# Attention, dense layer and expert layer on one core: first pair of heads loaded and split in parts, and a new table of order offsets for the attention

## The chip, the cores and the metric

The kernel runs on one core of a Trainium2 chip. The metric is the device time of one execution, in microseconds (us); lower is better. The core's engines run side by side, each through its own list of instructions in order: PE (TensorE, matrix products and transposes by an identity), DVE (VectorE), ACT (ScalarE), POOL (GpSimd) and SP (SyncE, which here only issues transfers, called DMAs).

## The reference

`q` has shape (2, 8, 1152, 64), and so have `k` and `v`: 2 batches of 8 heads. Two neighbouring rows of q are averaged, then plain softmax attention follows; its output is the input of a dense layer and that one's output the input of a layer with 8 experts.

```python
q_pool = q.reshape(B, H, S // factor, factor, D).mean(axis=3)
scores = scale * np.matmul(q_pool, k.transpose(0, 1, 3, 2))
scores = scores - np.max(scores, axis=-1, keepdims=True)
attn = np.exp(scores)
attn = attn / (np.sum(attn, axis=-1, keepdims=True) + 1e-09)
return np.matmul(attn, v).astype(np.float32)
...
h = x @ w_in
g = h - np.tanh(h)
return (g @ w_out).astype(np.float32)
```

## The kernel before

**Pairs and units.** The attention goes through 8 pairs of heads (c = 0 to 7). The 1152 pooled query rows of a pair make 9 units of 128 rows, numbered u = 9c + s; the unit s = 4 holds the last 64 rows of both heads.

**Preparation of a pair.** A DMA loads k of both heads (`ldk`), another q (`ldq`), another v (`ldv`). Each number of k and q is split into a high and a low half, since the products run in a format with fewer bits: for k a copy (`khi`) and a subtraction (`klo`) for each head, for q the addition of the two neighbouring rows (`qadd`), two copies (`qhi`) and a subtraction (`qlo`). All of these stand on POOL (helpers at L461, L470; L553). PE then transposes the halves into PSUM (`ktr` L534, `qtr` L570) and ACT copies them out (`kev`, `qev`, L459).

**A unit.** PE forms scores in three PSUM banks (`qk`, L664; there are two such sets of banks). DVE takes the row maximum (`max`, L670), ACT the exponential (`exp`, L678). POOL then splits the result into two 16-bit halves (`l` and `h`, L689), and one DMA transpose, issued from SP, puts both into the tile `pt` (`tr`, L694). For s = 3 and s = 7 the transposition is made on PE instead (`pT`, L706) with copies by ACT (L720) and DVE (L723).

**AV.** When a pair's transposes have landed, PE multiplies `pt` with v in six groups of 24 matmuls (`av{c}.{g}.{part}`, L736): g = 0 reads the columns of units 0, 1, 2, 4, 5, 6 of the pair, g = 1 those of units 2 to 4 and 6 to 8. There is one tile `pt`: the transposes of the next pair write over the same columns, so each waits for the AV groups that read them. After each g DVE scales the result (`xf`, L800), and POOL splits it for the next layer (`xhi`, `xlo`).

**Order.** Every operation is recorded with a due time `at`, to which the table `ORDER` adds an offset by the kind of operation. `Plan.run` then goes through all operations with assumed durations, gives each an engine, a place in the engine's list and its buffers, and writes the lists down; at run time nothing is reordered. Weights of the dense layer are loaded and split in the same lists (L851 to L880). The dense layer (L906, L963) and the experts come behind the attention.

Of the kernel before, what the change touches and what calls it, by code (L numbers as in the profile page):

```python
# [17 lines left out]
ALU = mybir.AluOpType  # L18
# [139 lines left out]
ORDER = {"av": -5.5, "c0": 12, "c1": 5, "c2": -6.5, "c3": -1.5, "cabs": -13.5, "kev": -2, "khi": -1.5, "klo": -6.5,  # L158
         "l": -4, "ldk": 0.5, "ldq": 2, "ldv": 1.5, "ldw": 3.5, "max": 0.5, "pth": 1.5, "ptl": 3, "qadd": -1.5,
         "qev": 13.5, "qhi": -2.5, "qk": -0.5, "qlo": -12, "qtr": 3, "rbe": -2, "rbt": 0.5, "rbz": 1, "rd": 8.5,  # L160
         "rec": 7.5, "rze": -4, "sv": 3, "tr": 18, "vbc": 3, "vhi": 1.5, "vlo": 11, "vsc": -2.5, "vsum": 0.5, "vtr": 6,
         "xf": -4.5, "xhi": -5, "xlo": -1.5}
# [248 lines left out]
def d1(n):  # L411
    return 0.12 + 0.00108 * n
# [6 lines left out]
def p2(n):  # L419
    return 0.2 + 0.0025 * n  # L420
# [6 lines left out]
class Kernel:  # L427
# [45 lines left out]

    def attention(self):
        nc, P = self.nc, self.P
        V = P.v
# [39 lines left out]

        def prep_k(n, need):
            raw = kraw[n // 2]

            def rw():  # L520
                return V(raw)[:, n % 2]

            sp = P.sb([KT, 2, D], F32R, f"ksp{n}")
            t = kT[n] = P.sb([S], F32R, f"kT{n}")
            P.op(self.copy_alts(lambda: V(sp)[:, :, 0, :], rw, KT * D, CFG["khi"], slow=True), r=[raw], w=[(sp, 0)],
                 at=need - CFG["kpr"], name=f"khi{n}")
            P.op(self.sub_alts(lambda: V(sp)[:, :, 1, :], rw, lambda: V(sp)[:, :, 0, :].bitcast(F32), KT * D, CFG["klo"]),
                 r=[raw, (sp, 0)], w=[(sp, 1)], at=need - CFG["kpr"] + 1, name=f"klo{n}")
            for g in range(3):
                ps = P.ps(1, F32R, f"kps{n}.{g}")  # L530

                def pe_(g=g, ps=ps):
                    for i in range(3):
                        nc.tensor.transpose(out=V(ps)[:, 0, i * 128:(i + 1) * 128],  # L534
                                            in_=V(sp)[:, 3 * g + i].rearrange("p a d -> p (a d)"), identity=ident_r)

# [5 lines left out]

        def prep_q(c, need):
# [15 lines left out]
            P.op(self.sub_alts(lambda: V(t)[:, :, 1, :], lambda: V(s), lambda: V(t)[:, :, 0, :].bitcast(F32), n, CFG["qlo"]),
                 r=[s, (t, 0)], w=[(t, 1)], at=need - CFG["qpr"] + 2, name=f"qlo{c}")  # L560
# [980 lines left out]
def sel(name, alts):  # L1541
# [9 lines left out]
           avg=2.7, av0=10.5, avs=2.0, fin=11.5, t1=21, hp=8.1, wld=8, wcv=20, wsp=17, cv0=60, cvs=25, fn0=2, hch=6, xadd='ppvppvppv', xof=6,  # L1551
# [56 lines left out]
```

## Time and profile before

| | |
|---|---|
| time, 3 runs | 654.37 us median, 652.66 to 654.85 |
| the profiled execution | 655.12 us, of it the span in the trace 653.1 us |
| PE busy over the span | 588.3 us, 90% |
| DVE, ACT, POOL busy | 373.9, 349.8 and 348.0 us |
| chain that ended last | issue 15%, one DMA behind the dense layer 5% |

The profile's span runs from the first to the last instruction of the program. Busy time of an engine leaves out issuing, branches and waits. A row of the timeline gives the start, the time to the last end of the merged instructions, the engine, the line of the code, output and input with their shapes, the count, and in brackets the idle time before it and the instruction that ended it.

### The profile page before, as it was taken

To read this page: it belongs to the slowest core of one execution; us is meant where nothing else is said; L and a number is where in the kernel's file an instruction comes from. 1 tells how busy PE (TensorE), PEld (TensorE's weight loads), DVE (VectorE), ACT (ScalarE), POOL (GpSimd) and SP (SyncE) were. 2 spreads that over 40 slices of the span, in tenths; PEclk is the share of its full clock that TensorE was granted. 3 is DMA by queue.
4 is the path that set the end of the run, shared out by engine and by line. 5 is a ranking of instruction groups with operands and counts; after the bars stand their busy time and mean duration, and the time that the engine had idled before them with its cause. 6 is when DMAs were issued, how large, how long until landed. Compare 5 with 4: busy or idle time off the path is not lost. (4 is left out here: it accounts for less than half of the span.)

```text
span 653.1 us, 10491 instructions
## 1 busy us (share of the span) xinstructions
PE 588.3 (90%) x3840; PEld 471.9 (72%) x3840; DVE 373.9 (57%) x579; ACT 349.8 (54%) x641; POOL 348.0 (53%) x303
## 2 busy tenths in 40 slices
PE   3879898979898979999999999899999959999993
PEld 2767787867786868888899999799989456338331
DVE  1687767695777686898879896854554021101100
ACT  4886877776868786856775766544441100120011
POOL 7996959696969588976446365522232100110111
PEclk9979999998999999999999999899998979999997
DMA  7799989998999695999935123344277843595000
GB/s 217 167 200 204 218 195 204 219 212 172 192 214 211 128 176 124 162 349 356 411 131 178 34 67 95 119 139 129 67 215 249 224 128 129 178 371 190 22 24 13
DMA packets 172371, 114.82 MB, mean 176 GB/s; under 512 B 135470, under 2 KB 144686, under 8 KB 172048
## 3 DMA queue, kind: packets, MB, share of 16 engines
q1 hardware_dynamic: 169152, 109.37, 64.5%
q0 software_dynamic: 1680, 3.81, 1.9%
q10 hardware_dynamic: 1472, 0.79, 0.6%
q8 instruction: 37, 0.61, 0.4%
q14 instruction: 30, 0.25, 0.1%
HBM read 66.22 MB, written 16.15 MB: 126 GB/s over the span
## 5 line engine op out<-in xcount | busy, mean ns | idle before, releaser
L470 POOL TENSOR_TENSOR b<-b,b 128x512 fp32r<-128x512 f32 (+2 forms) x88 | 149.9, 1715 | 97.8 <-ACT b L459 80.6
L689 POOL TENSOR_SCALAR b<-b 128x1152 f16<-128x1152 uint16 (+1 forms) x110 | 131.5, 1216 | 42.1 <-ACT b L678 37.8
L963 PE MATMUL psum<-b,b 128*128 128x512 f32 x432 | 118.3, 400 | 4.3 <-POOL b L470 3.7
L670 DVE CUSTOM_DVE_ANT_1 b<-psum,na 128x1152 f16<-128x1152 f32 x72 | 97.5, 1355 | 42.5 <-PE psum L664 34.8
L906 PE MATMUL psum<-b,b 128*128 128x384 f32 x576 | 116.0, 340 | 1.0 <-DVE b L723 1.0
L906 PEld LDWEIGHTS psum<-b,b 128*128 128x128 f32 x576 | 103.8, 190 | 8.3 <-DVE b L723 1.3
L678 ACT ACTIVATE b<-psum,b 128x1152 int32<-128x1152 f32 (+1 forms) x72 | 88.0, 1222 | 39.3 <-DVE b L670 36.2
L664 PE MATMUL psum<-b,b 128*128 128x384 f32 x384 | 87.5, 365 | 18.0 <-ACT b L678 17.3
L963 PEld LDWEIGHTS psum<-b,b 128*128 128x128 f32 x432 | 79.5, 189 | 17.9 <-POOL b L470 5.4
L664 PEld LDWEIGHTS psum<-b,b 128*128 128x128 f32 x384 | 67.3, 197 | 26.6 <-ACT b L678 21.5
L459 ACT ACTIVATE b<-psum 128x384 fp32r<-128x384 f32 (+3 forms) x119 | 60.2, 540 | 46.1 <-PE psum L963 14.6
L736 PE MATMUL psum<-b,b 128*64 128x288 f16 x1152 | 81.1, 293 | 3.7 <-DMA b<-b 1.4
L736 PEld LDWEIGHTS <-b 128*64 128x64 f16 x1152 | 64.9, 112 | 15.7 <-issue 10.4
L459 ACT ACTIVATE b<-b 128x512 fp32r<-128x512 f32 (+1 forms) x56 | 39.7, 720 | 48.3 <-DVE b L937 25.8
L1270 POOL DMA_INDIRECT out_dram<-b,b x8 | 7.3, 916 | 80.2 <-DVE b L1424 40.2
L1424 DVE SCALAR_TENSOR_TENSOR b<-psum,b,b 64x512 f32<-64x512 f32 x8 | 5.9, 742 | 70.1 <-ACT b L1421 70.1
L1404 ACT ACTIVATE b<-psum 128x512 f32<-128x512 f32 x8 | 4.8, 597 | 58.6 <-PE psum L1400 58.6
L878 DVE SCALAR_TENSOR_TENSOR b<-b,b 128x512 uint32<-128x512 uint32 x32 | 34.7, 1101 | 0.2
L929 DVE SCALAR_TENSOR_TENSOR b<-psum,b 128x768 f32<-128x768 f32 x24 | 22.8, 952 | 17.3 <-ACT b L924 8.2
L880 DVE SCALAR_TENSOR_TENSOR b<-b,b 128x512 uint32<-128x512 uint32 x32 | 32.4, 1026 | 0.2
L1389 PE MATMUL psum<-b,b 128*64 128x512 f32 x128 | 30.6, 602 | 2.0 <-ACT b L459 1.4
L723 DVE SCALAR_TENSOR_TENSOR b<-psum,b 128x384 f16<-128x384 f32 x48 | 25.0, 551 | 12.1 <-ACT b L720 12.1
(130 smaller groups left out, 803.2 us busy)
## 6 DMA issues: line engine op xcount, KB each, us to landing
b<-in_moe_w_dram SPq DMA_DIRECT2D x64, 512.0 KB, 6.0
b<-in_moe_w_in_dram SPq DMA_DIRECT2D x32, 256.0 KB, 4.4
b<-in_moe_w_out_dram SPq DMA_DIRECT2D x16, 512.0 KB, 7.5
xs<-b SPq DMA_DIRECT2D x6, 771.0 KB, 9.9
b<-in_k_dram SPq DMA_DIRECT2D x8, 576.0 KB, 4.2
b<-in_q_dram SPq DMA_DIRECT2D x8, 576.0 KB, 5.4
b<-in_v_dram SPq DMA_DIRECT2D x8, 576.0 KB, 4.2
xd<-b SPq DMA_DIRECT2D x2, 2304.0 KB, 18.0
```

The source lines that it names most:

```text
L459: "a": ("act", (a_ps if ps else a_sb)(n), lambda: nc.scalar.activation(out=dst(), in_=src(), func=ACTF.Copy)),
L470: "p": ("pool", p2(n), lambda: nc.gpsimd.tensor_tensor(out=dst(), in0=a(), in1=b(), op=ALU.subtract)),
L664: nc.tensor.matmul(out=V(S_)[:, j, 0:CB], lhsT=lhsT, rhs=rhs[:, j * CB:(j + 1) * CB], start=(m == 0), stop=(m == len(mm) - 1))
L670: P.op([("dve", 1.43, lambda: nc.vector.tensor_tensor_reduce(out=V(junk), in0=V(S_)[:, :, 0:CB], in1=self.na[:, 3:4].unsqueeze(2).to_broad ...
L678: P.op([("act", 1.4, lambda: nc.scalar.activation(out=V(p).rearrange("p (a e) -> p a e", a=3), in_=V(S_)[:, :, 0:CB], func=ACTF.Exp, bias= ...
L689: P.op([("pool", p1(S), lambda a=a, src=src, by=by: nc.gpsimd.tensor_scalar(out=V(hl)[:, a], in0=src(), scalar1=by, scalar2=0.0, op0=ALU.m ...
L736: nc.tensor.matmul(out=V(ps)[i * D:(i + 1) * D, 0, 0:half], lhsT=V(v16[2 * c + i])[:, j, vl, :], rhs=V(pt)[:, hl * KT + j, i * SQ + g * ha ...
L878: (0.9, lambda: nc.vector.scalar_tensor_tensor(out=V(t), in0=lo(), scalar=29, in1=V(t), op0=ALU.logical_shift_right, op1=ALU.bitwise_or)),
L880: (0.9, lambda: nc.vector.scalar_tensor_tensor(out=V(t), in0=hi(), scalar=0x80000000, in1=V(t), op0=ALU.bitwise_and, op1=ALU.bitwise_or)),
L906: nc.tensor.matmul(out=V(h)[:, a, 0:384], lhsT=w, rhs=V(xx)[:, dk, sl], start=(n == 0), stop=(n == 11))
L963: nc.tensor.matmul(out=V(ps)[:, 0, :], lhsT=V(g[gi, blk, i][gl])[:, a, sl], rhs=V(wo[2 * gi + i, a])[:, wl, :], start=(i == 0 and a == 0 a ...
L1389: nc.tensor.matmul(out=V(h)[i * SM:(i + 1) * SM, 0, :], lhsT=V(xT[e // 2])[:, e % 2, k], rhs=V(w[e, k])[:, i * FH:(i + 1) * FH], start=(k ...
```

## The change

For pair 0 alone, k is loaded by one DMA for each head and q by two (blocks 0 to 4, then 5 to 8), issued k, q, k, q. Head 0 of k and the first part of q no longer go through POOL alone: copies on ACT, addition and subtraction on DVE. Pair 0's transposed tiles are copied out of PSUM by DVE or ACT. The table `ORDER` is replaced, and five numbers of the due times (`av0`, `avs`, `fin`, `cv0`) with it, which applies to all pairs.

```diff
-ORDER = {"av": -5.5, "c0": 12, "c1": 5, ... "qadd": -1.5, ... "xlo": -1.5}
+ORDER = {"av": -4, "c0": 15.5, "c1": -5.5, ... "qadd": -3, ... "xlo": -1}
...
+    def add_alts(self, dst, a, b, n, engs="vp"):
+        nc = self.nc
+        c = {
+            "v": ("dve", d1(n), lambda: nc.vector.tensor_tensor(out=dst(), in0=a(), in1=b(), op=ALU.add)),
+            "p": ("pool", p2(n), lambda: nc.gpsimd.tensor_tensor(out=dst(), in0=a(), in1=b(), op=ALU.add)),
+        }
+        return [c[e] for e in engs]
...
+            if c == 0:
+                for i in range(2):
+                    P.op([("dma", 1.45, lambda i=i: nc.sync.dma_start(
+                        out=V(raw)[:, i].rearrange("p j d -> p (j d)"), in_=k[b, h + i].rearrange("(p j) d -> p (j d)", j=KT)))],
+                        w=[(raw, i)], at=need - CFG["kld"] + 3 * i, name=f"ldk{c}.{i}")
+                return
...
+            khi, klo, kev = ("a", "v", "va") if n == 0 else (CFG["khi"], CFG["klo"], CFG["kev"])
...
+            first = c == 0
+            for pt, (t0, t1) in enumerate(((0, NF + 1), (NF + 1, NS)) if first else ((0, NS),)):
...
+                early = first and pt == 0
+                qadd, qhi, qlo = ("v", "a", "v") if early else (CFG["qadd"], CFG["qhi"], CFG["qlo"])
...
-                P.op([("pe", len(blocks) * 0.105, pe_)], r=[t], w=[ps], at=at, name=f"qtr{c}.{gi}")
+                P.op([("pe", len(blocks) * 0.105, pe_)], r=tr, w=[ps], at=at, name=f"qtr{c}.{gi}")
...
-           avg=2.7, av0=10.5, avs=2.0, fin=11.5, t1=21, hp=8.1, wld=8, wcv=20, wsp=17, cv0=60, ...
+           avg=2.7, av0=9.5, avs=3, fin=12, t1=21, hp=8.1, wld=8, wcv=20, wsp=17, cv0=55, ...
```

The order of instructions changes on every engine from the first load to the last AV. On PE the lists of both kernels agree again from the dense layer on, but for a few neighbours.

On PE, at the start of the program, before the change: b_115 and b_117 are the halves of k of heads 0 and 1, b_143 those of q of pair 0, b_130 and b_177 the transposed k and q, b_164 and b_231 the same of pair 1.

```order
L534 MATMUL psum<-ident_r,b_115 128x128 x9
L534 MATMUL psum<-ident_r,b_117 128x128 x9
L605 MATMUL psum<-ident,b_141 2x128
L570 MATMUL psum<-ident_r,b_143 128x128 x18
L664 MATMUL psum<-b_130,b_177 128x384 x6
L627 MATMUL psum<-b_184,ones 128x4
L664 MATMUL psum<-b_130,b_177 128x384 x6
```

The same place with the change: b_115 and b_143 are the halves of k of heads 0 and 1, b_133 those of q, b_125 and b_149 the transposed k and q.

```order
L549 MATMUL psum<-ident_r,b_115 128x128 x9
L594 MATMUL psum<-ident_r,b_133 128x128 x10
L688 MATMUL psum<-b_125,b_149 128x384 x12
L549 MATMUL psum<-ident_r,b_143 128x128 x6
L688 MATMUL psum<-b_125,b_149 128x384 x6
L594 MATMUL psum<-ident_r,b_133 128x128 x8
L629 MATMUL psum<-ident,b_192 2x128
```

Head 1 of k, the second part of q and the step for v (L605, now L629) have gone from ahead of the first scores to between the units.

On POOL, from the first load to the halves of unit 0 (L689), before: the list goes through k and q of pair 0 (b_111, b_113) and of pair 1 (b_137, b_159) and then reaches unit 0.

```order
L461 TENSOR_SCALAR b_115<-b_111 128x9x64
L461 TENSOR_SCALAR b_117<-b_111 128x9x64
L470 TENSOR_TENSOR b_115<-b_111,b_115 128x9x64
L553 TENSOR_TENSOR b_122<-b_113 128x576
L470 TENSOR_TENSOR b_117<-b_111,b_117 128x9x64
L461 TENSOR_SCALAR b_143<-b_122 128x9x64 x2
L470 TENSOR_TENSOR b_143<-b_122,b_143 128x9x64
...
L461 TENSOR_SCALAR b_231<-b_198 128x9x64 x2
L470 TENSOR_TENSOR b_231<-b_198,b_231 128x9x64
L689 TENSOR_SCALAR b_261<-b_241 128x1152 x2
L689 TENSOR_SCALAR b_285<-b_264 128x1152 x2
```

With the change (L713 is L689 of before, L478 stands for L553): head 1 of k and the second part of q, then unit 0; pair 1 (b_204, b_184) follows between the units.

```order
L461 TENSOR_SCALAR b_143<-b_111 128x9x64
L470 TENSOR_TENSOR b_143<-b_111,b_143 128x9x64
L478 TENSOR_TENSOR b_128<-b_113 128x256
L461 TENSOR_SCALAR b_133<-b_128 128x4x64 x2
L470 TENSOR_TENSOR b_133<-b_128,b_133 128x4x64
L713 TENSOR_SCALAR b_202<-b_186 128x1152 x2
L713 TENSOR_SCALAR b_221<-b_200 128x1152 x2
L478 TENSOR_TENSOR b_241<-b_204 128x576
L713 TENSOR_SCALAR b_252<-b_233 128x1152 x2
L461 TENSOR_SCALAR b_280<-b_241 128x9x64 x2
L470 TENSOR_TENSOR b_280<-b_241,b_280 128x9x64
L461 TENSOR_SCALAR b_301<-b_184 128x9x64
```

Eight instructions of pair 1 that stood ahead of unit 0 now stand behind it, up to unit 6.

On SP, the transposes of pair 2 up to the one before its AV, before: b_298 is the tile `pt`, the first two rows belong to units 18 and 19, the last four to units 20, 22, 23 and 24.

```order
L694 DMA_TRANSPOSE b_298<-b_900 128x18x128
L694 DMA_TRANSPOSE b_298<-b_944 128x18x128
L851 DMA b_1151<-in_moe_w_in_dram 128x256 x2
L596 DMA b_1184<-in_v_dram 128x2x576
L694 DMA_TRANSPOSE b_298<-b_1091 128x18x128
L694 DMA_TRANSPOSE b_298<-b_1182 128x18x128
L694 DMA_TRANSPOSE b_298<-b_1243 128x18x128
L694 DMA_TRANSPOSE b_298<-b_1268 128x18x128
```

The same six transposes with the change (L718 is L694 of before, b_266 the tile `pt`).

```order
L718 DMA_TRANSPOSE b_266<-b_884 128x18x128
L718 DMA_TRANSPOSE b_266<-b_919 128x18x128
L571 DMA b_1141<-in_q_dram 128x9x128
L718 DMA_TRANSPOSE b_266<-b_1021 128x18x128
L718 DMA_TRANSPOSE b_266<-b_1130 128x18x128
L718 DMA_TRANSPOSE b_266<-b_1183 128x18x128
L718 DMA_TRANSPOSE b_266<-b_1231 128x18x128
```

Two loads of weights and one of v have left the place ahead of the last four transposes; one load of q stands there.

## Rows read from the trace of the kernel before

**Rows 1.** Waits of PE up to 290 us: total us, times, longest us.

```profile
PE psum L664 <- ACT b L678: 17.6, 21, 1.9
PE psum L736 <- DMA b<-b: 1.4, 2, 0.8
```

**Rows 2.** Busy us of each engine by stage, then PE's granted clock, DMA share, GB/s.

```profile
0.00:17.10 17.10, 6.40 (x37) 5.02 (x38) 2.72 (x12) 7.04 (x16) 13.67 (x38) 1.00 0.72 208
17.10:51.40 34.30, 27.99 (x158) 24.86 (x157) 27.78 (x43) 28.57 (x58) 33.25 (x29) 0.90 0.90 191
...
286.40:494.90 208.50, 204.22 (x1039) 182.86 (x1040) 153.25 (x197) 116.91 (x185) 97.52 (x57) 0.99 0.50 170
```

**Rows 3.** The same columns, stretches from a pair's last AV group to the next pair's first.

```profile
68.52:83.55 15.03, 11.43 (x78) 9.71 (x77) 11.35 (x23) 13.87 (x28) 13.69 (x13) 1.00 1.07 202
...
166.44:179.63 13.19, 11.01 (x77) 9.80 (x75) 9.55 (x21) 12.86 (x28) 12.56 (x13) 0.95 1.03 185
...
261.52:276.30 14.78, 13.72 (x81) 12.77 (x81) 13.31 (x20) 13.14 (x26) 14.17 (x11) 1.00 0.98 169
sum 104.54, PE 84.64 PEld 75.03 DVE 83.25 ACT 90.93 POOL 98.55; mean PE 12.09 PEld 10.72 DVE 11.89 ACT 12.99 POOL 14.08
```

**Rows 4.** The same columns, stretches from a pair's first AV group to its last.

```profile
51.44:68.52 17.08, 16.45 (x184) 13.37 (x183) 11.78 (x19) 9.63 (x19) 11.63 (x11) 1.00 0.96 215
...
sum 130.37, PE 128.32 PEld 107.97 DVE 84.63 ACT 88.01 POOL 88.16; mean PE 16.04 PEld 13.50 DVE 10.58 ACT 11.00 POOL 11.02
```

**Rows 5.** Timeline of PE from 160 to 170 us, end of pair 3's AV.

```profile
164.78 1.66 PE L736 MATMUL psum<-b,b 128*64 128x288 f16 x24
```

**Rows 6.** Timeline of SP from 164 us, transposes of pair 4.

```profile
166.60 11.25 SPq L694 DMA_TRANSPOSE b<-b  x4
```

**Rows 7.** The instructions of L694 from 166.7 to 177.8 us, their landing.

```profile
DMA to landing us min/median/max: 4.7/4.8/4.9
```

**Rows 8.** Timeline of all engines, from the first load to AV of pair 0.

```profile
1.29 0.49 SPq L513 DMA_DIRECT2D b<-in_k_dram  x1
...
5.59 1.31 POOL L461 TENSOR_SCALAR b<-b 128x576 fp32r<-128x576 f32 x2 [2.46 <-DMA b<-in_k_dram]
...
8.31 1.00 PE L534 MATMUL psum<-ident_r,b 128*128 128x128 f32 x6 [8.31 <-POOL b L470]
...
17.10 2.25 PE L664 MATMUL psum<-b,b 128*128 128x384 f32 x6
...
20.98 1.65 DVE L642 SCALAR_TENSOR_TENSOR b<-b,b,b 128x576 f16<-128x576 f32 x1
...
22.90 7.24 POOL L689 TENSOR_SCALAR b<-b 128x1152 f16<-128x1152 uint16 x6 [0.88 <-ACT b L678]
...
23.83 0.82 DVE L642 SCALAR_TENSOR_TENSOR b<-b,b,b 128x576 f16<-128x576 f32 x1
...
38.40 5.53 POOL L689 TENSOR_SCALAR b<-b 128x1152 f16<-128x1152 uint16 x4
...
54.87 1.31 PE L664 MATMUL psum<-b,b 128*128 128x384 f32 x6
```

**Rows 9.** Groups by line and form up to 290 us: busy us, mean ns, idle before.

```profile
L670 DVE CUSTOM_DVE_ANT_1 b<-psum,na 128x1152 f16<-128x1152 f32 x72 | 97.5, 1355 | 42.5 <-PE psum L664 34.8 <-ACT b L678 2.7 <-ACT b L873 2.6
L678 ACT ACTIVATE b<-psum,b 128x1152 int32<-128x1152 f32 x56 | 68.4, 1221 | 25.9 <-DVE b L670 22.9 <-POOL b L689 1.2 <-POOL b L470 1.2
L689 POOL TENSOR_SCALAR b<-b 128x1152 f16<-128x1152 uint16 x56 | 67.8, 1210 | 42.1 <-ACT b L678 37.8 <-issue 3.2 <-DMA b<-b 0.3
L470 POOL TENSOR_TENSOR b<-b,b 128x576 fp32r<-128x576 f32 x32 | 46.6, 1457 | 0.9
L461 POOL TENSOR_SCALAR b<-b 128x576 fp32r<-128x576 f32 x40 | 27.3, 693 | 5.4 <-DMA b<-in_k_dram 2.8 <-DVE b L800 1.8 <-POOL b L689 0.7
L459 ACT ACTIVATE b<-psum 128x512 fp32r<-128x512 f32 x32 | 18.7, 597 | 2.4 <-PE psum L570 2.1 <-DVE b L642 0.2
L601 ACT ACTIVATE b<-b 128x576 f16<-128x576 f32 x16 | 10.9, 684 | 0.0
```

More of the change, by code (lines that the diff above doesn't have):

```diff
@@ L155, in cost @@
     return d
[L158 to L162, printed above, removed]
+ORDER = {"av": -4, "c0": 15.5, "c1": -5.5, "c2": -9.5, "c3": 0.5, "cabs": -14.5, "exp": 3, "h": 1.5, "kev": -2,
+         "khi": 5, "klo": -9.5, "ktr": -1, "l": -2.5, "ldk": 1, "ldq": 1.5, "ldv": 1.5, "ldw": -6, "pth": 4.5,
+         "ptl": 4.5, "qadd": -3.5, "qev": 18.5, "qhi": 10, "qk": -2.5, "qlo": -8, "qtr": 11.5, "rbe": -5, "rbt": -1.5,
+         "rbz": -1, "rd": 7.5, "rec": -3, "rze": -6, "sv": 13.5, "tr": 13.5, "vbc": 3.5, "vlo": 9.5, "vsc": -5.5,
+         "vsum": -5.5, "vtr": 6, "xf": -6.5, "xhi": 13, "xlo": -1}
 def kind(name):
@@ L524, in prep_k @@
             t = kT[n] = P.sb([S], F32R, f"kT{n}")
-            P.op(self.copy_alts(lambda: V(sp)[:, :, 0, :], rw, KT * D, CFG["khi"], slow=True), r=[raw], w=[(sp, 0)],
+            khi, klo, kev = ("a", "v", "va") if n == 0 else (CFG["khi"], CFG["klo"], CFG["kev"])
+            P.op(self.copy_alts(lambda: V(sp)[:, :, 0, :], rw, KT * D, khi, slow=True), r=[(raw, n % 2)], w=[(sp, 0)],
                  at=need - CFG["kpr"], name=f"khi{n}")
-            P.op(self.sub_alts(lambda: V(sp)[:, :, 1, :], rw, lambda: V(sp)[:, :, 0, :].bitcast(F32), KT * D, CFG["klo"]),
-                 r=[raw, (sp, 0)], w=[(sp, 1)], at=need - CFG["kpr"] + 1, name=f"klo{n}")
+            P.op(self.sub_alts(lambda: V(sp)[:, :, 1, :], rw, lambda: V(sp)[:, :, 0, :].bitcast(F32), KT * D, klo),
+                 r=[(raw, n % 2), (sp, 0)], w=[(sp, 1)], at=need - CFG["kpr"] + 1, name=f"klo{n}")
             for g in range(3):
@@ L565, in prep_q @@
                 ps = P.ps(1, F32R, f"qps{c}.{gi}")
+                tr = [(t, (int(gi > 2) if first else None, j)) for j in range(3)]
                 blocks = [(g[0], s_ + g[1] * (NF + 1)) for s_ in range(NF)] if g != "z" else [(0, NF), (1, NF)]
@@ L573, in prep_q @@
                 at = need - CFG["qtr"] + gi
-                P.op([("pe", len(blocks) * 0.105, pe_)], r=[t], w=[ps], at=at, name=f"qtr{c}.{gi}")
+                P.op([("pe", len(blocks) * 0.105, pe_)], r=tr, w=[ps], at=at, name=f"qtr{c}.{gi}")
                 if g != "z":
                     P.op(self.copy_alts(lambda g=g: V(qt)[:, g[0], g[1] * NF:(g[1] + 1) * NF, :].rearrange("p a e -> p (a e)"),
-                                        lambda ps=ps: V(ps)[:, 0, :].bitcast(F32), 512, CFG["qev"], True),
+                                        lambda ps=ps: V(ps)[:, 0, :].bitcast(F32), 512, "va" if first else CFG["qev"], True),
                          r=[ps], w=[(qt, g)], at=at + 0.3, name=f"qev{c}.{gi}")
```

32 lines of the change are left out of this document (18 added, 14 removed).

## The prediction

> **What bounds the kernel now.** I read the table of stages first. Up to 17.10 us PE is busy for 6.40 us, since it waits for the first k and q; in the dense layer, from 286.4 us on, it is busy for 204.22 of 208.50 us [rows 2]. That layer's list on PE stays as it is, so it moves with the attention's end, and the change is worth what it takes from the attention.
>
> The list of waits alone would mislead: PE's largest sum is 17.6 us for `exp` to give back a set of score banks, and only 1.4 us are put down to transposes [rows 1]. The timeline around a pair's AV shows the loop that sets the pace. The last AV group of pair 3 starts at 164.78 us and takes 1.66 us [rows 5]; at 166.60 SP issues the first of four transposes that had to wait for it [rows 6]; four take 11.25 us to issue, 2.8 us each, and the last one's landing comes 4.8 us behind its own issue [rows 7]: 166.60 + 3 x 2.8 + 4.8 = 179.8, and AV of the next pair starts at 179.63 [rows 3]. So a pair lasts as long as its AV phase plus this chain. The eight AV phases take 130.37 us and PE is busy in 128.32 of them [rows 4]: bound by PE. The seven stretches between them take 104.54 us, PE being busy for 84.64 [rows 3]: bound by the chain, except the last, 14.78 us, which PE fills with the dense layer's first products. The first six average (104.54 - 14.78) / 6 = 14.96 us, the shortest is 13.19.
>
> So two things can shorten the attention: an earlier first AV, and shorter stretches.
>
> **The change part by part.** *First scores.* Before: whole k issued at 1.29, used at 5.59; POOL makes both heads' halves and q's; first scores at 17.10 [rows 8]. Now the chain is head 0 and five ninths of q. Landing of the half of k: 5.6 if splitting brings nothing, 3.4 if all of the 4.3 us went with the bytes; I take 5.0, nearer to no gain, as issue and completion do not shrink. `khi` on ACT 0.68 [rows 9], to 5.7. `klo` on DVE: the two-input row at L642 took 0.82 once and 1.65 once [rows 8]; with 0.82, 6.6 after hand-over. Three groups of transposes at 0.5 (six took 1.00 [rows 8]). Meanwhile DVE has in its list a copy from PSUM (0.45, scaled from 0.597 for 512 columns [rows 9]), `qadd` (0.82 x 5/9 = 0.46), a second copy, and `qlo` 0.46 behind ACT's first `qhi` (0.38): 7.2, 7.7, 8.1, 8.6, 9.1. Then eight transposes of q at 0.17, 10.5, and a copy out, 0.6: 11.1; with some 0.03 us for each of ten hand-overs, **11.4 instead of 17.1**. With k at 5.6 and the DVE rows at 1.65 it is 13.4, with k at 3.4 it is 9.8.
>
> The trace has a reason to doubt DVE's price: L642 took 1.65 while POOL ran a two-input row, and 0.82 while it ran one-input rows [rows 8]. The Trainium skill (GPSIMD Engine Reference, section 1. Specifications) says that GpSimd shares its SBUF interfaces with VectorE and contends with DVE instructions that have two SBUF inputs, which speaks against spreading such work over DVE and POOL at once. By that rule `qadd` and `qlo`, which meet POOL's share of the work, cost 0.93 each instead of 0.46, the first scores come at 12.3, and the sum below is 0.9 us smaller.
>
> *First softmax halves on POOL.* Scores 1.31 to 2.25, `max` 1.36, `exp` 1.22 [rows 8, 9], ACT no longer held by v's copies: l0 starts at 16.0 instead of 22.90, 6.9 earlier. POOL's own rows ahead of it (head 1, rest of q: 0.69 + 1.46 + 1.3 + 0.6 = 4.1) end near 11, hidden behind the scores; without that cover l0 would slip by what they overrun.
>
> *What moves behind.* POOL's four additions and subtractions and four copies for pair 1 now stand between the units. From l0 to h6 the new list has 11 halves at 1.21, four two-input rows at 1.457 and four copies at 0.693 [rows 9]: 21.9 us, so h6 ends at 37.9. Before, it ended at 38.40 + 5.53 = 43.93 [rows 8]. The same method gives 12 x 1.21 + 3 x 1.457 + 3 x 0.693 = 21.0 for before, where the trace has 21.03.
>
> *First AV.* Its last transposes follow h6: 37.9 + 4.8 = 42.7 at the earliest. On PE 13 units stand ahead of it instead of 12; 12 took from 17.10 to 51.40, 2.86 each [rows 2], so at the old pace 11.4 + 37.2 = 48.6. That pace holds a clock granted at 0.90 on the mean [rows 2] and waits for POOL, which may or may not recur; neither bound is nearer, so I take 46.0: **5.4 us earlier** than 51.44 [rows 4], with 2.8 and 8.7 as bounds.
>
> *Pair 0's AV phase.* One unit's scores, 1.31 [rows 8], have left it: **1.3 us**. At its end the fourth transpose (unit 15) has its turn 8.5 us later, at about 69.2 us; POOL's list to h15 (23 halves, 12 two-input rows, 11 copies, 52.9 us from 16.0 on) ends at 68.9. So POOL has 0.3 us to spare here: this is where the moved work can bite.
>
> *Later pairs.* PE's content of the AV phases is the same within a unit (one unit more in pair 2's, one transpose group more in two others). Ahead of the four transposes SP has a load or two less in pairs 1 and 2, and no weights in their midst in pair 5. Bounds: no gain, or all five shorter stretches at 13.19, 5 x 1.8 = 9 us. I take **1.0 us** in all, close to no gain, as the stretch of 13.19 is one of six. The copies for z on DVE, `h` of five units on ACT and the weights' earlier due times lie beside these loops; uncovered, `h` costs ACT 1.2 us each.
>
> **Sum:** 5.4 + 1.3 + 1.0 = 7.7. The profiled execution took 655.12 us, so 647.4; it lies 0.7 above the median of the runs shown, 654.37, from which the sum gives 646.7. I say 647. About 0.3%, 2 us, is what a measurement can tell from no change.
>
> **The rivals.** *The lead is eaten by POOL: no change.* POOL was busy for 33.25 of 34.30 us from the first scores to the first AV [rows 2], and it now begins that stretch with pair 1's halves still to form. Where `exp` must wait for a buffer that POOL still reads, the units keep POOL's pace, AV starts near the late bound, and h15 misses its turn by as much as POOL lost: lead 2.8 + 1.3, less 3 at unit 15: 654. It decides once h15 comes 3 us or more behind its turn. Against it: POOL's list to h6 ends 6 us sooner by rows, and the waits of `exp` for POOL sum to 2.4 us [rows 9].
>
> *The new lists lengthen the chain in every pair: slower.* The fourth transpose needs h of the pair's seventh unit (s = 6). In the new lists its scores start right behind AV's end: 1.31 + 1.36 + 1.22 + 2 x 1.21 = 6.3 us, against the turn at 8.5. ACT has `h` of the unit before, 1.2, and copies of k ahead of that `exp`, and POOL has `xhi`, `qadd`, `xlo`, 3.6 us, which begin only when DVE has scaled AV's result. If these cost more than 2.2 us, each of the six stretches grows by the rest; at 1.3 us the lead is gone, at 2 us the time is 655.1 - 6.7 + 12 = 660. Against it: in the lists of before, the same rows of POOL stand ahead of the same halves, and the shortest stretch is still 13.19.
>
> *More than forecast.* If AV starts at 43.5 and the stretches come to 14 us, the gain is 7.9 + 1.3 + 5 x 0.96 = 14: 641.
>
> *The parts land no earlier than the whole:* 0.6 us less than the sum, within the forecast's range.
>
> **How the numbers follow.** Forecast, 643 to 651: 0.62. More: 0.15, all faster. Eaten lead, 651 to 656: 0.13, of it 0.02 below 652.4. Longer chain: 0.10. Faster 0.62 + 0.15 + 0.02 = 0.79; slower, the longer chain alone, 0.10; same 0.11. The range must take in the eaten lead and most of the gain: 640 to 655.5 leaves out the longer chain and the far end of the larger gain, some 0.15.
>
> **What would show it.** Right: first scores at 10 to 13 us, l0 near 16, first AV between 43 and 49, stretches between AV phases of 13 to 15 us, and the dense layer starting 6 to 10 us sooner and as long as before. Wrong: first AV past 50 us; waits of `tr` for POOL in the stretch behind pair 0; stretches of 16 us or more; or PE in the dense layer waiting for weights that the earlier start finds not yet split.

## The result and the profile after

The changed kernel took 645.58 us (median of 3 runs, 645.41 to 647.35) against 654.37: ratio 0.988, 95% interval 0.9842 to 0.9918. In a second comparison with more runs (twelve against 35) it took 646.91 against 652.15, ratio 0.9922, 0.9888 to 0.9956; medians hold all runs, while ratios leave out a run that is over 1.5% longer than the fastest of its kernel. I take the second: 0.8%, 5 us faster. The forecast was 647.0 and faster; but the place where the forecast put the gain, the first AV, did not move.

The timeline of the changed kernel, from the first load to the first AV, answers to [rows 8] (L549 is L534 of before, L594 is L570, L688 is L664, L702 is L678, L713 is L689, L760 is L736):

```profile
4.59 0.68 ACT L459 ACTIVATE b<-b 128x576 fp32r<-128x576 f32 x1 [2.52 <-DMA b<-in_k_dram]
5.31 0.76 DVE L469 TENSOR_TENSOR b<-b,b 128x576 fp32r<-128x576 f32 x1 [2.39 <-ACT b L459]
6.12 1.00 PE L549 MATMUL psum<-ident_r,b 128*128 128x128 f32 x6 [6.12 <-DVE b L469]
...
7.25 0.48 DVE L477 TENSOR_TENSOR b<-b 128x320 f32<-128x320 f32 x1
...
8.53 0.59 DVE L469 TENSOR_TENSOR b<-b,b 128x320 fp32r<-128x320 f32 x1
...
11.00 3.57 PE L688 MATMUL psum<-b,b 128*128 128x384 f32 x12
...
16.18 1.15 POOL L713 TENSOR_SCALAR b<-b 128x1152 f16<-128x1152 uint16 x1 [3.54 <-ACT b L702]
...
36.48 1.16 POOL L713 TENSOR_SCALAR b<-b 128x1152 f16<-128x1152 int16 x1
...
45.49 2.44 POOL L713 TENSOR_SCALAR b<-b 128x1152 f16<-128x1152 uint16 x2
...
49.45 0.48 ACT L459 ACTIVATE b<-psum 128x384 fp32r<-128x384 f32 x1
49.60 2.07 PE L688 MATMUL psum<-b,b 128*128 128x384 f32 x6
51.60 1.66 PE L760 MATMUL psum<-b,b 128*64 128x288 f16 x24
```

The start is as forecast: first scores at 11.00 (forecast 11.4, before 17.10), the first half on POOL at 16.18 (forecast 16.0, before 22.90), and the second half of unit 6, h6, ends at 36.48 + 1.16 = 37.64 (forecast 37.9, before 43.93). And yet AV begins at 51.60, where it began before (51.44): from first scores to first AV it now takes 40.6 us instead of 34.3.

The table of stages of the changed kernel: the stretch ahead of the first AV, the last us of it, two stretches between AV phases and their sum, the first AV phase and the sum of all eight (columns as in [rows 2]):

```profile
11.00:51.60 40.60, 32.63 (x170) 29.02 (x169) 27.46 (x50) 32.25 (x67) 36.80 (x36) 0.83 0.93 193
...
44.00:52.00 8.00, 8.00 (x37) 6.99 (x39) 7.34 (x11) 6.39 (x16) 8.00 (x8) 0.57 1.07 190
...
66.43:81.53 15.10, 11.63 (x78) 10.23 (x78) 10.95 (x24) 13.18 (x27) 13.18 (x13) 1.00 0.99 197
97.70:111.06 13.36, 10.74 (x78) 9.66 (x77) 10.43 (x23) 12.18 (x22) 13.09 (x13) 1.00 0.98 179
...
sum 101.27, PE 81.50 PEld 72.91 DVE 76.03 ACT 85.96 POOL 94.46; mean PE 11.64 PEld 10.42 DVE 10.86 ACT 12.28 POOL 13.49
...
51.60:66.43 14.83, 14.83 (x175) 12.01 (x175) 11.18 (x15) 10.24 (x21) 10.68 (x9) 1.00 0.87 223
...
sum 130.02, PE 127.23 PEld 105.25 DVE 95.14 ACT 94.27 POOL 88.20; mean PE 15.90 PEld 13.16 DVE 11.89 ACT 11.78 POOL 11.03
```

Against [rows 3] the stretches are 3.3 us shorter in sum, against [rows 4] pair 0's AV phase is 2.25 us shorter and the eight together the same. Ahead of the first AV several things are full at once: PE is busy for 8.00 of 8.00 us from 44 to 52 at a mean clock of 0.57, POOL as well, and the DMA share is 1.07. Attention ends at 282.89 instead of 286.35 us, 3.5 us earlier. As the span is 9.3 us shorter, more than half of the difference between these two profiles lies behind the attention, where the prediction expected none.

### The profile page after: what moved, and what is told of

The parts are those of the page before. It is cut to its first block, busy times and chain, and to the rows that moved or that the text cites. A ratio compares the mean times of both kernels' runs of the same rounds, so it can differ in the third digit from the quotient of the medians.

```text
span 643.8 us, 10541 instructions
## 1 busy us (share of the span) xinstructions
PE 582.0 (90%) x3840; PEld 466.3 (72%) x3840; DVE 391.9 (61%) x595; ACT 349.6 (54%) x634; POOL 335.1 (52%) x298
## 5 line engine op out<-in xcount | busy, mean ns | idle before, releaser
L470 POOL TENSOR_TENSOR b<-b,b 128x576 fp32r<-128x576 f32 (+2 forms) x87 | 140.1, 1619 | 105.2 <-ACT b L459 68.5
L713 POOL TENSOR_SCALAR b<-b 128x1152 f16<-128x1152 int16 (+1 forms) x107 | 127.9, 1216 | 39.1 <-ACT b L702 29.9
L694 DVE CUSTOM_DVE_ANT_1 b<-psum,na 128x1152 f16<-128x1152 f32 x72 | 97.6, 1355 | 43.2 <-PE psum L688 29.1
L702 ACT ACTIVATE b<-psum,b 128x1152 int32<-128x1152 f32 (+1 forms) x72 | 87.9, 1222 | 30.8 <-DVE b L694 24.3
L688 PE MATMUL psum<-b,b 128*128 128x384 f32 x384 | 87.2, 366 | 13.1 <-ACT b L702 12.1
L760 PE MATMUL psum<-b,b 128*64 128x288 f16 x1152 | 79.5, 288 | 3.5 <-DVE b L747 2.3
L688 PEld LDWEIGHTS psum<-b,b 128*128 128x128 f32 x384 | 68.1, 199 | 17.1 <-ACT b L702 14.8
L459 ACT ACTIVATE b<-psum 128x384 fp32r<-128x384 f32 (+3 forms) x114 | 58.3, 534 | 39.2 <-PE psum L987 13.2
L760 PEld LDWEIGHTS <-b 128*64 128x64 f16 x1152 | 62.4, 110 | 15.8 <-issue 10.5
L459 ACT ACTIVATE b<-b 128x512 fp32r<-128x512 f32 (+3 forms) x59 | 40.8, 711 | 49.5 <-DVE b L961 30.1
L1006 DVE TENSOR_TENSOR b<-b,b 128x512 f32<-128x512 f32 x14 | 23.2, 1659 | 21.3 <-ACT b L459 21.3
L904 DVE SCALAR_TENSOR_TENSOR b<-b,b 128x512 uint32<-128x512 uint32 x32 | 34.2, 1083 | 0.1
L958 DVE SCALAR_TENSOR_TENSOR b<-b,b 128x768 f32<-128x768 f32 x24 | 30.1, 1256 | 4.6 <-ACT b L951 3.2
L1413 PE MATMUL psum<-b,b 128*64 128x512 f32 x128 | 30.6, 602 | 2.1 <-DMA b<-in_moe_w_dram 1.5
L1438 PE MATMUL psum<-b,b 128*64 128x512 f32 x128 | 29.2, 596 | 2.4 <-PEq L1516 1.6
```

What stands on the lines that cost most here:

```text
L459: "a": ("act", (a_ps if ps else a_sb)(n), lambda: nc.scalar.activation(out=dst(), in_=src(), func=ACTF.Copy)),
L470: "p": ("pool", p2(n), lambda: nc.gpsimd.tensor_tensor(out=dst(), in0=a(), in1=b(), op=ALU.subtract)),
L688: nc.tensor.matmul(out=V(S_)[:, j, 0:CB], lhsT=lhsT, rhs=rhs[:, j * CB:(j + 1) * CB], start=(m == 0), stop=(m == len(mm) - 1))
L694: P.op([("dve", 1.43, lambda: nc.vector.tensor_tensor_reduce(out=V(junk), in0=V(S_)[:, :, 0:CB], in1=self.na[:, 3:4].unsqueeze(2).to_broad ...
L702: P.op([("act", 1.4, lambda: nc.scalar.activation(out=V(p).rearrange("p (a e) -> p a e", a=3), in_=V(S_)[:, :, 0:CB], func=ACTF.Exp, bias= ...
L713: P.op([("pool", p1(S), lambda a=a, src=src, by=by: nc.gpsimd.tensor_scalar(out=V(hl)[:, a], in0=src(), scalar1=by, scalar2=0.0, op0=ALU.m ...
```

## The experiments

In those from loads_early on, the lists of the changed kernel are planned as they were and then altered by name just ahead of being written down: nothing is laid out anew. `MOVE` holds (what, which other, 0 for ahead of it, 1 for behind it), `OFF` new places in SBUF. The table gives what the profiles and the runs showed, us; ratios are to runs of the kernel before on the same chip.

| run | first AV | pair 0's AV ends | attention ends | time, median | ratio (95%) |
|---|---|---|---|---|---|
| before, two profiles | 51.44, 51.76 | 68.52, 67.96 | 286.35, 287.45 | | |
| changed, two profiles | 51.60, 52.49 | 66.43, 68.28 | 282.89, 286.30 | 646.91 | 0.9922 (0.9888, 0.9956) |
| structure_alone | 55.60 | 74.12 | 301.16 | 670.26 | 1.0286 (1.0235, 1.0337) |
| table_alone | 50.10 | 66.71 | 293.01 | 659.21 | 1.0104 (1.0065, 1.0142) |
| loads_early | 51.69 | 67.39 | 284.60 | 645.85 | 0.9881 (0.9837, 0.9925) |
| fill | 54.20 | 69.03 | 284.38 | 649.01 | 0.9961 (0.9922, 0.9999) |
| av0_ahead | 50.30 | 67.69 | 285.33 | 646.28 | 0.9926 (0.9892, 0.9959) |
| fill2 | 51.86 | 68.47 | 284.06 | 645.93 | 0.9919 (0.9888, 0.9950) |
| all_three | 50.00 | 67.54 | 283.31 | 647.42 | 0.9944 (0.9910, 0.9979) |
| p10_apart | 46.98 | 64.81 | 285.90 | 646.98 | 0.9899 (0.9828, 0.9971) |
| klo_dve | 46.74 | 64.23 | 283.07 | 644.97 | 0.9874 (0.9807, 0.9941) |
| late_start | 58.70 | 74.13 | 291.26 | 653.78 | 1.0035 (0.9995, 1.0074) |

**The two halves of the change.** (The change has four due times, not five, and its table has `qadd` at -3.5.)

```diff
 structure_alone: open loads, halves and copies as changed
-ORDER = {"av": -4, "c0": 15.5, ...}   av0=9.5, avs=3, fin=12, cv0=55
+ORDER = {"av": -5.5, "c0": 12, ...}   av0=10.5, avs=2.0, fin=11.5, cv0=60
 table_alone: loads, halves and copies as before
-ORDER = {"av": -5.5, "c0": 12, ...}   av0=10.5, avs=2.0, fin=11.5, cv0=60
+ORDER = {"av": -4, "c0": 15.5, ...}   av0=9.5, avs=3, fin=12, cv0=55
```

> The parts of pair 0's loads and their split on three engines, with the table ORDER and the five due times of the kernel before. Theory of the prediction (the gain is the earlier start, carried through the first AV into the attention's end): first scores near 11 us, first AV 3 us or more ahead of 51.44, time 646 to 649. Rival (the first AV is held by PE's list and by half clock ahead of it, and the gain comes from the table: from AV phases, from stretches and from the order in the dense layer): first scores near 11 us all the same, first AV within 2 us of 51.44, dense layer from the attention's end to the routing as long as before, time 651 to 654.

> The kernel before with the new table ORDER and the five new due times; pair 0 is loaded whole and split on POOL as before. Theory of the prediction: first scores near 17 us as before, first AV near 51 us, time 652 to 654, as the table alone was worth 1 to 2 us. Rival (the gain comes from the table): the attention ends 2 us or more earlier although its start does not, the dense layer has no stretch at half clock near 415 us, time 647 to 650.

Both theories missed: each half alone is slower than the kernel before, by 2.9% and 1.0%, though structure_alone has its first scores at 10.93. The stages tell where. Two stretches between AV phases of structure_alone, then one of table_alone and one of its AV phases:

```profile
137.96:156.06 18.10, 13.09 (x95) 11.36 (x93) 13.90 (x27) 14.64 (x32) 17.93 (x16) 1.00 0.86 174
172.29:195.45 23.16, 18.12 (x105) 15.78 (x105) 19.08 (x32) 17.39 (x36) 22.79 (x21) 0.93 0.68 132
```

```profile
195.16:217.21 22.05, 17.03 (x109) 14.56 (x108) 16.71 (x30) 16.87 (x36) 20.52 (x20) 1.00 0.85 170
245.27:268.67 23.40, 20.11 (x196) 16.86 (x195) 14.44 (x25) 14.81 (x28) 17.09 (x16) 0.93 0.65 124
```

POOL fills the stretch of 23.16 us (busy 22.79): in that list preparation of a later pair stands between the halves whose transposes AV waits for. In that time SP's transposes wait 20.3 us for POOL. This is the rival of the longer chain, with a table that belongs to another start. In table_alone POOL is busy for 20.52 of 22.05 us; what makes its AV phase of 23.40 us so long was not followed up. The two halves of the change don't add up: this table is a gain only together with these operations.

**Transfers.** Four loads leave the midst of pair 0's transposes.

```diff
+MOVE = (("ldv1", "ldq1", 1), ("ldk2", "ldv1", 1), ("ldq2", "ldk2", 1), ("ldw0.0", "ldq2", 1))
+OFF = {"vraw1": 96768, "kraw2": 101376, "qraw2": 105984, "raw0.0": 110592}
```

> The changed kernel with four loads taken out of the midst of pair 0's transposes: v of pair 1, k and q of pair 2 and one weight tile are put into SBUF that is empty at that time and are issued right behind q of pair 1, while the DMA engines have little to do (share 0.32 at 15 to 20 us). Everything else stands in the same order. Theory that transfers hold the first AV (DMA share 1.0 to 1.2 from 20 to 50 us, transposes issued 4.1 to 4.6 us apart instead of 2.8): the seventh transpose of pair 0 is issued near 39.5 instead of 42.74, and first AV moves from 51.60 to 48 to 49, time 2 to 3 us shorter. Rival (PE's own list and its clock hold it): the transposes come earlier as well, but first AV stays within 1 us of 51.60 and the time within 1 us of the changed kernel's.

The timeline of SP in loads_early: seven transposes in a row, issued by 44.49 instead of 49.0; the sixth, the last that the first AV group needs, at 38.59 instead of 42.74 (the expectation calls it the seventh).

```profile
18.15 26.34 SPq L729 DMA_TRANSPOSE b<-b  x7
44.59 0.54 SPq L631 DMA_DIRECT2D b<-in_v_dram  x1
```

The first AV stays at 51.69: the rival holds; transfers alone don't keep it back.

**PE's order and its clock.** `fill` and `fill2` add products that nobody reads (in the text of `fill`, 34 should read 25: 9, 5 and 11); `av0_ahead` moves one AV group.

```diff
 fill:      +FILL = {2: (9, 5), 3: (11, 0), 8: (0, 14), 10: (6, 0)}  # products into a score bank's unused columns
            +KFILL = {(3, 0): 10}                                    # transposes behind a ktr, in its bank
 fill2:     +FILL = {2: (0, 5)}  +KFILL = {(1, 1): 8, (1, 2): 10, (3, 0): 10}  +QFILL = {(1, 2): 12}
 av0_ahead: +MOVE = (("av0.0.0", "qk12", 0),)
```

> The changed kernel with 55 more matmuls of 128x128 whose result nobody reads, put on PE ahead of instructions that wait there between 15 and 44 us (34 of them ahead of unit 3's scores or by 18 us, 30 between 36 and 44 us), each bundle shorter than the wait that it fills. Theory that half clock holds the units ahead of the first AV: PE's clock is no longer granted half at 20.6 to 27.4 and 44.5 to 51.3, units 3 and 4 take 1.3 and 2.4 us instead of 2.29 and 4.08, units 10 to 12 take 1.3 instead of 1.9 to 2.25, first AV comes at 47.5 to 49, the attention ends 2 to 3 us earlier, and the time is 642.5 to 644. Rival (transfers hold it): the clock may stay up, but first AV still comes past 50.5 and the time stays within 1 us of the changed kernel's.

> The changed kernel with 45 transposes and matmuls of 128x128 that nobody reads, this time in PSUM banks that PE need not wait for: 8 and 5 and 10 of them between 15 and 20.9 us, 12 and 10 between 36.6 and 42.8, each bundle ahead of an instruction that waits there. Theory that half clock costs the units ahead of the first AV: clock not half between 20.6 and 27.4 nor between 44.4 and 51.3, units 3 and 4 at 1.3 and 2.4 us instead of 2.29 and 4.08, first AV at 48 to 49.5, attention's end 2 us or more earlier, time 642 to 644. Rival (another chain holds the units, the exponential and its buffers): the clock stays up, PE waits the longer for the exponential, first AV within 1 us of 51.60, time within 1 us of the changed kernel's.

> The changed kernel with one thing moved on PE: pair 0's first group of 24 AV matmuls stands ahead of unit 12's scores instead of behind them. Theory that PE's own work holds this stretch (PE busy 5.00 of 5.00 us from 45 to 65): first AV comes 1.5 to 2.5 us earlier, at 49 to 50, but the last AV of pair 0 stays at 66.4 and the time within 1 us of the changed kernel's; so an earlier first AV is by itself worth nothing. Rival (the prediction's step: each us by which AV starts earlier is a us at the end): attention's end 1.5 to 2 us earlier and the time 643.5 to 644.

`fill` does not test its theory, and its first AV (54.20) and time (649.01) are nobody's forecast. Its first products write columns of a score bank that the exponential does not read, and waited for it all the same, so that they lengthened the chain; a row of its PE:

```profile
16.16 1.22 PE L690 MATMUL psum<-ident_r 128*128 128x128 f32 x9 [1.08 <-ACT b L715]
```

`fill2`, in other banks, did what it should: clock 1.00 from 20 to 40 us and 0.99 from there to 49, unit 3 at 1.31 us instead of 2.29 and unit 4 at 2.38 instead of 4.08. But PE then waited longer. Its timeline ahead of the first AV:

```profile
44.54 1.35 PE L704 MATMUL psum<-b,b 128*128 128x384 f32 x6
45.73 0.37 PE L556 MATMUL psum<-ident_r,b 128*128 128x128 f32 x3
46.36 0.45 PE L556 MATMUL psum<-ident_r,b 128*128 128x128 f32 x3 [0.25 <-ACT b L466]
49.65 2.29 PE L704 MATMUL psum<-b,b 128*128 128x384 f32 x6 [2.84 <-ACT b L719]
51.86 3.09 PE L777 MATMUL psum<-b,b 128*64 128x288 f16 x24
```

PE is through with unit 11 by 46 us and waits 2.84 us for unit 10's exponential: the rival holds, half clock up to 49 us was not what held the first AV. `av0_ahead` moved the first AV by 1.3 us (expected 1.5 to 2.5), and neither the end of that AV phase (67.69) nor the time with it, as the theory of a full PE has it. But PE was not full here; the AV group stood 2.47 us for a copy on ACT:

```profile
50.30 3.16 PE L768 MATMUL psum<-b,b 128*64 128x288 f16 x24 [2.47 <-ACT b L467]
```

**All of these at once, and what was still in the way.**

```diff
 all_three: the MOVE and OFF of loads_early, the MOVE of av0_ahead, the products of fill2
 p10_apart: all_three and
+MOVE += (("kev4.0", "exp10", 0),)     OFF += {"p10": 12800}
 klo_dve:   p10_apart and
+ON_DVE = ("klo2", "klo3", "klo4", "klo5")
```

> The changed kernel with the four loads issued early, the first AV group ahead of unit 12's scores, and the 45 unread products between 15 and 43 us, all at once. Theory that loads, PE's order and half clock together hold the first AV: first AV at 45 to 47 (the seventh transpose lands near 46), attention's end at 279 to 280.5 instead of 282.89, time 641 to 643. Rival (the pace of the later pairs is set by their own chains, so that a start 4 us earlier is lost by pair 2): first AV at 45 to 48, attention's end within 1 us of 282.89, time within 1 us of the changed kernel's.

First AV at 50.00 missed both ranges; the attention's end, 283.31, and the time are the rival's. The timeline of all_three, POOL and ACT ahead of its first AV:

```profile
43.89 1.61 POOL L494 TENSOR_TENSOR b<-b 128x576 f32<-128x576 f32 x1
45.48 2.74 POOL L739 TENSOR_SCALAR b<-b 128x1152 f16<-128x1152 uint16 x2
...
48.26 1.22 ACT L728 ACTIVATE b<-psum,b 128x1152 int32<-128x1152 f32 x1 [2.10 <-POOL b L739]
...
49.47 0.48 ACT L475 ACTIVATE b<-psum 128x384 fp32r<-128x384 f32 x1
50.00 2.83 PE L786 MATMUL psum<-b,b 128*64 128x288 f16 x24 [3.92 <-ACT b L475]
```

Read from the end: AV waits for a bank, which the copy at 49.47 gives back (one of pair 2's k). The copy stands on ACT behind unit 10's exponential at 48.26. That one writes into the place of unit 9's tile and waits for POOL to have split it, 45.48 to 48.22. And these halves stand on POOL behind pair 2's work, `qadd2` at 43.89 and both halves of k ahead of it. So the time gained at the start was filled with work of pair 2.

> The kernel of the run before (loads early, first AV group ahead of unit 12's scores, unread products on PE) with two more edits: the tile that the exponential of unit 10 writes lies in SBUF that is empty instead of in the place of unit 9's, and one copy of pair 2's k out of PSUM, whose bank the first AV group takes over, stands ahead of that exponential on ACT instead of behind it. Theory that POOL holds the first AV: unit 9's halves stand on POOL behind pair 2's halves of k and addition of q and end at 48.2, the exponential of unit 10 waits 2.1 us for them, the copy and the AV group behind it; so unit 10's exponential now starts near 46.2 and first AV comes at 46 to 47.5 instead of 50.0. If a lead at the first AV reaches the end, the attention ends at 280 to 281.5 and the time is 2 us shorter than that run's 647.4; if the later chains lose it, the attention ends within 1 us of 283.3. Rival (something else holds it, transfers or v's halves): first AV stays past 49.

With these two waits taken out, first AV comes at 46.98, a us from the prediction's 46.0; the timeline of p10_apart:

```profile
46.45 0.48 ACT L475 ACTIVATE b<-psum 128x384 fp32r<-128x384 f32 x1
46.83 1.22 ACT L728 ACTIVATE b<-psum,b 128x1152 int32<-128x1152 f32 x1
...
46.98 1.73 PE L786 MATMUL psum<-b,b 128*64 128x288 f16 x24 [0.52 <-ACT b L475]
...
57.64 2.27 POOL L739 TENSOR_SCALAR b<-b 128x1152 f16<-128x1152 uint16 x2 [1.55 <-ACT b L728]
64.03 1.41 POOL L494 TENSOR_TENSOR b<-b 128x576 f32<-128x576 f32 x1 [4.13 <-DMA b<-in_q_dram]
```

But only the AV group moved. POOL's list behind it is no earlier, it even waits 4.13 us for q of pair 3, whose load stands where it stood; the stretch behind pair 0 grows from 15.10 to 17.68 us, at a mean clock of 0.85 instead of 1.00. Pair 1's AV starts at 82.49, later than in the changed kernel (81.53), the attention ends at 285.90 and the time is the changed kernel's within the interval. A first AV 4.6 us earlier is lost within one pair; how much of that is q and how much the clock was not told apart. (In klo_dve, the next run, q costs only 0.56 us: there 1.1 of 4.9 us are left at pair 1's AV, 80.47, and none at the attention's end.) (The end was expected at 280 to 281.5, or within 1 us of 283.3; it is later than both, at a mean clock of 0.974 against 0.985 in all_three.)

> As the run ahead of this one, and the four subtractions of k of pairs 1 and 2 (1.43 us each on POOL) stand on DVE, in the same places of the program's order. Theory that POOL's work bounds units 4 to 15 (busy 5.00 of 5 us in nearly every slice from 20 to 55): the halves of units 6, 9 and 12 come 2.9, 4 and 5 us earlier, units follow, pair 0's last AV group ends 2 us or more earlier, and the attention ends 2 to 3 us earlier than in the run ahead. Rival (DVE, which has about 1.3 us to spare in 5, becomes the bound in POOL's place, with 0.8 to 1.65 us for each subtraction; or the chain of transposes in later pairs takes the lead back): the attention ends within 1 us of the run ahead, or later.

POOL's halves of unit 9 end at 44.95 instead of 48.64 (42.32 + 2.63 against 45.89 + 2.75), and the attention at 283.07, 2.8 us ahead of p10_apart, as the first theory had it; pair 0's last AV group ended only 0.6 us earlier, though, where it said 2 or more. The theory is not shown by this, since 17.9 us of p10_apart's profile were lost to half clock against 13.3, and the ratios overlap.

**The start by itself.** Nine needless copies on ACT hold back the chain to the first scores.

```diff
+            for x in range(9 if o.name == "khi0" else 0):
+                self.slow()
...
+                P.slow = lambda: nc.scalar.activation(out=V(sp)[:, :, 1, :], in_=rw(), func=ACTF.Copy)
```

> The changed kernel with nine needless copies of head 0 of k on ACT, 0.68 us each, ahead of the copy that starts the chain to the first scores (what they write is overwritten); nothing else is moved. So the first scores start as late as in the kernel before, near 17 us instead of 11.0. Theory of the prediction (each us of the start is a us at the first AV and at the end): first AV near 57, attention's end 5 us or more later than the 282.9 and 286.3 of the two profiles of the changed kernel, time 651.5 to 653 against 646.9 for the changed kernel. Theory from the runs so far (a shift of the first AV between 46.7 and 54.2 us left the attention's end between 283 and 286.3; POOL's work and the transposes set the pace of pairs 0 to 2): first AV at 53 to 57, attention's end at 283 to 288, time 646.5 to 649.5.

The prediction's theory was right here (the time, 653.78, a little past its 651.5 to 653), and the one from the runs so far wrong. The timeline of late_start:

```profile
17.09 3.23 PE L693 MATMUL psum<-b,b 128*128 128x384 f32 x12
...
22.19 4.50 POOL L718 TENSOR_SCALAR b<-b 128x1152 f16<-128x1152 uint16 x4 [3.48 <-ACT b L707]
...
58.70 2.27 PE L765 MATMUL psum<-b,b 128*64 128x288 f16 x24
```

Scores come 6.1 us later, POOL's first half 6.0, the first AV 7.1 or 6.2 (against the two profiles), the attention's end 8.4 or 5.0. Half clock does not explain it: 14.0 us of PE time are lost to it in this profile, as in the first of the changed kernel. Taken through the kernel before, the time is 1.0035 - 0.9922 = 1.1%, some 7 us, longer, and the intervals don't touch; by medians it is 5.0 us (653.78 against 654.05 for the kernel before on the same chip, where the changed kernel had 646.91 against 652.15). So in these lists the earlier start is worth about as many us as it is earlier, and without it the changed kernel is no faster than the one before (0.9995 to 1.0074).

**The same kernels once more.**

> The changed kernel once more, in more rounds against the kernel before. Theory that part of the 8.8 us between the medians is stretches at half clock, which fall differently from execution to execution (before: 20.2 us lost to half clock in the profiled execution, of it 1.4 us at the end of the routing and about 1.7 at 417 us on the path; changed kernel: 14.0): the medians lie 5 to 7 us apart, and runs of one kernel with 0.01 more granted clock on the mean are 3 to 5 us shorter. Rival (the difference is all in the lists of instructions): the medians lie 8 to 10 us apart again, and the time does not go with the clock.

> The kernel before, profiled once more, to tell what of its stages is the program and what the clock of one execution. Theory that the 5.8 us between the stages behind the attention (366.7 against 360.9 us) are in part half clock: this execution has no half clock at the end of the routing, that stage lasts 2.9 us instead of 4.27, and all behind the attention 362 to 365.5 us. Rival (all in the lists): 366 to 367.5 us again.

The medians lay 5.2 us apart, as the first theory said. In the 30 runs of before that the ratio holds (646.68 to 654.71 us) a straight line through time and mean granted clock falls by 3.9 us for each 0.01 of clock (correlation -0.75), again as it said; for the changed kernel it is 2.2 us at a correlation of only -0.38. The two profiles of the changed kernel differ by 3.4 us in the attention alone (282.89, 286.30), with 14.0 and 17.6 us of PE time lost to half clock over the profile. So attention's ends within 3 us of each other tell nothing by themselves, and from the second profile of each, before and changed, the attention itself has gained 287.45 - 286.30 = 1.2 us, from the first 3.5. The stages behind the attention (dense layer; gate and counts; up to the experts' first wide products; the rest), before_again and then after_again:

```profile
287.45:494.63 207.18, 203.78 (x1039) 183.03 (x1040) 153.56 (x197) 116.58 (x185) 98.48 (x57) 0.99 0.50 170
494.63:502.03 7.40, 7.11 (x65) 6.72 (x63) 3.25 (x15) 2.01 (x4) 1.31 (x1) 1.00 0.95 323
502.03:547.47 45.44, 36.60 (x197) 26.64 (x197) 7.05 (x20) 3.67 (x6) 4.63 (x5) 0.92 0.52 150
547.47:651.90 104.43, 91.52 (x366) 41.29 (x364) 11.86 (x17) 12.55 (x20) 10.89 (x12) 0.98 0.40 143
```

```profile
286.30:493.38 207.08, 203.23 (x1044) 182.05 (x1044) 165.81 (x198) 116.28 (x185) 93.60 (x58) 1.00 0.50 169
493.38:499.99 6.61, 6.61 (x63) 6.50 (x61) 3.36 (x15) 0.82 (x2) 1.62 (x2) 1.00 0.92 307
499.99:542.89 42.90, 35.67 (x194) 26.29 (x195) 7.34 (x20) 3.67 (x6) 4.64 (x5) 0.92 0.57 172
542.89:647.25 104.36, 91.52 (x366) 41.29 (x364) 11.86 (x17) 12.56 (x20) 10.90 (x12) 0.97 0.41 143
```

Behind the attention before_again takes 364.45 us (first profile 366.72), after_again 360.95 (first 360.89). The dense layer is equally long; 0.8 us are gained at the gate, where the last tiles' logits stand earlier in PE's list, and 2.5 us up to the experts' first wide products, where PE's waits are put down to DVE (3.7 us) and a transfer (3.3) before, and to transfers alone (7.2) with the change. Which line of the new order does the latter was not tried.

## Why the prediction was right in its number and wrong in a step

- **First scores and first halves: right.** 11.00, 16.18 and 37.64 us against 11.4, 16.0 and 37.9. The prices held: `qadd` 0.48 and `qlo` 0.59 (forecast 0.46 each) on DVE, `khi` 0.68 on ACT. The doubt about DVE's price was hardly put to the test: POOL's first row of pair 0 started at 8.12, behind `qadd`, and its subtraction at 8.86, beside the end of `qlo`. (By the prediction's own rows the late bound of this step is 13.8 and not 13.4.) The first part of k was in use at 4.59, between the bounds of 3.4 and 5.6 and 0.4 ahead of the value taken.
- **"I take 46.0: 5.4 us earlier than 51.44": this step failed.** First AV came at 51.60 and 52.49, past the 50 us that the prediction named as the sign of an error. It took h6 as the last thing needed and scaled the pace of the units. It left out that the new lists put pair 2's halves and addition on POOL ahead of unit 9's halves, that unit 10's exponential needs unit 9's place, and that the bank of the AV group comes free behind that exponential. The term's size was right only for another list: without these two waits, with loads early, the AV group ahead of unit 12 and unread products for the clock (46.98 in p10_apart). Its meaning was wrong: there it is worth nothing at the end. In the changed kernel that chain ends with ACT's copy at 49.93, and PE's 13 units, partly at half clock, at 51.60; transfers came close too, so that taking away any one left the first AV within 1.5 us of 51.6, or later.
- **"An earlier first AV" as the way from the start to the end: wrong; the start's worth: right.** Late_start shows 5 to 7 us for 6 us of start. What it shifts is the whole list, on POOL from its first half on (busy 36.80 of 40.60 us ahead of the first AV), not the AV group alone. The lead of the start has become more work done ahead of the first AV, given back in a shorter AV phase of pair 0 (forecast 1.3; measured 2.25 in the first profiles, 0.4 in the second) and shorter stretches (forecast 1.0 in all; 3.3 in the first profiles, 1.1 in the second). At the spot where the prediction gave POOL 0.3 us to spare, unit 15's turn is by its own rows 70.3 and not 69.2, so 1.4 us; the stretch there stayed as long as it was (15.10 against 15.03).
- **"The dense layer as long as before": right; that nothing else behind the attention moves: wrong.** 3.5 us by the second profiles (364.45 against 360.95), 5.8 by the first, of which 1.4 were half clock in the routing of before (twenty products there took 3.89 us and in before_again 2.48) and 1.5 lie in the dense layer, with its wait and half clock at 417 us.
- **The sum** of 7.7 us stands against about 5. By stages its largest term, 5.4, came out at nothing, and 3.5 us or more came from behind the attention, where it had nothing: that the sum came out near is partly luck. Late_start shows what the rest of the change does. With first scores at 17.09, as before, its first AV comes at 58.70, 7 us later than before: the new lists put that much more ahead of it. They give it back behind, 232.6 us from first AV to attention's end against 234.9 and 235.7 before, and 361.2 from there on against 366.7 and 364.5. The earlier start is what makes up for the 7 us.
- **The rivals.** "The lead is eaten by POOL" had the right engine and the right direction for the first AV (later even than its late bound, 48.6), but it too took the first AV for the gain. "The new lists lengthen the chain" is what happens to either half of the change alone.

## What to carry to other kernels

A lead is worth something at the end when all that stands behind it in the lists of the engines moves with it; to price an early start, delay it on purpose, and don't move a single milestone. (Such a delay tells what these lists would lose, not what others would gain.) Where order comes from a planner with a table of offsets, table and operations are one edit: measured apart both were losses here. Look also for buffers taken over from the unit before: a wait for a place in SBUF or a bank shows in no list of instructions, and two of them in a row tied this AV to another pair's preparation.

## What the runs showed of the chip that I had not expected

The same kernel spreads over 8 us (before: 646.68 to 654.71), along with the mean granted clock, 0.971 to 0.986. In the profiles PE's clock falls to half, 1.2 GHz, for 3.4 to 10.2 us at a time, but not at the same places in each: at 417 us in the first profile of before (behind a wait of 1.66 us for POOL), not there in the second.

DVE's price for a two-input row next to POOL was as uneven as before the change. The four subtractions of klo_dve (128x576 on DVE):

```profile
28.96 0.85 DVE L489 TENSOR_TENSOR b<-b,b 128x576 fp32r<-128x576 f32 x1
...
31.94 1.72 DVE L489 TENSOR_TENSOR b<-b,b 128x576 fp32r<-128x576 f32 x1
...
36.76 0.75 DVE L489 TENSOR_TENSOR b<-b,b 128x576 fp32r<-128x576 f32 x1
...
41.35 1.47 DVE L489 TENSOR_TENSOR b<-b,b 128x576 fp32r<-128x576 f32 x1
```

The fourth ran beside POOL's addition of 1.40 us, which has two inputs. The Trainium skill (GPSIMD Engine Reference, section 1. Specifications) says that GpSimd contends with DVE instructions that have two SBUF inputs. The trace agrees, and not only where POOL's row has two inputs as well: the one of 1.72 ran mostly beside POOL's 16-bit halves, which have one input, and the one of 0.75 beside nothing on POOL. The one of 0.85 ran beside one-input rows too, the later of which, a half, took 1.64 us instead of 1.15; there, it seems, POOL was the one that waited. The prediction's two rows, 1.65 beside two inputs and 0.82 beside one [rows 8], were too few to tell these cases apart: in the same trace the rows of 1.52 and 1.47 us at 180.77 and 182.43 (L642) lie wholly beside halves.
